# Order of the first loads, and one repeated weight load, in a two-problem attention kernel

## The chip, the cores and the metric

The kernel runs on one core of a Trainium2 chip. The metric is the device time of one execution in microseconds (us); lower is better. Times are medians over several runs unless a profiled execution is named, which is a single run.

## The reference

Two problems of the same shape, A and B, are computed one after the other and their outputs are joined along the last axis. All tensors are bf16. Each has tokens x (16 x 32 x 1024), a key and a value cache (16 x 4 x 512 x 128) and two weight matrices.

```python
q = (x @ wq).reshape(B, Sq, Hq, Dh).transpose(0, 2, 1, 3)   # 32 heads of 128
k = jnp.repeat(k_cache, rep, axis=1)                        # 4 kv heads, each for 8
v = jnp.repeat(v_cache, rep, axis=1)
scores = jnp.einsum("bhqd,bhkd->bhqk", q, k) * (Dh ** -0.5)
p = softmax(scores)
o = jnp.einsum("bhqk,bhkd->bhqd", p, v)
return o.transpose(0, 2, 1, 3).reshape(B, Sq, Hq * Dh) @ wo
```

## The kernel before

The 512 tokens of a problem (16 x 32) are four tiles of 128. The width of 1024 is eight chunks of 128 (`DC` = 8); `HC` is half of them, 4. There are 32 query heads in four groups of 8 (`REP`), one group for each key/value head.

**The head of the kernel** (L456 to L557) computes the queries of the first eight heads of problem A. It is the only stage in which the tensor engine has no other work. Six heads (`NF`) have their sums in PSUM first, the last two join later. The first four chunks of x are loaded as rows into `x_sb` and turned by tensor-engine transposes (`transpose_x`, L515, instructions at L519) with a copy out by VectorE for the one chunk and ScalarE for the other (L523); the last four chunks come through DMA transposes (`load_x_transposed`, L471). The weights of the eight heads come through `load_w0` (L477), piece by piece: first chunk 0 and chunk 1 of six heads, each 192 KB, from ScalarE's queue, then all others from SyncE's. The tokens are loaded by `load_x` (L465): two pieces of 128 KB (token tiles 0-1 and 2-3 of chunks 0 and 1), then one of 256 KB (chunks 2 and 3).

While these arrive, the tensor engine runs 23 matmuls on constants (`warm_up`, L509), whose result is not used. The written order after that is: transposes of the first half of the tokens, three more such matmuls, chunk 0 of three heads over the first half, transposes of the second half, chunk 0 of the other three heads, and so on (L537 to L557).

**What follows on SyncE's queue.** Behind the head's loads come block (0, 2) of the query weights, keys of group 0, block (0, 3), keys of group 1 and values of groups 0 and 1 (L496 to L501). A block `(pr, c4)` is 1 MB: all chunks of four heads, from head 4 x c4, of problem `pr`; `load_wq` (L242) allocates a new tile and enters it into `wq_tiles[pr, c4]`. The queue takes one DMA after another. Each DMA uses one of eight semaphores in turn, so that a DMA also waits for the one that used its semaphore last.

**The main loop** has 128 slots (i = 0 to 127), one for each pair of batch and key/value head of the two problems. A slot computes its scores (L358), the exponential on ScalarE (L366), sums on VectorE (L377) and, five slots later, the product with the values (L426). Between these the tensor engine takes about seven units of a stream of projection matmuls (`stream`, L559): eight units make a query head (L302), 32 make a tile of output (L321). Five units run before slot 0 (L576), and each slot runs 1, 5 and 1 of them, every fourth slot one less. Loads for later slots are entered in a plan and issued at the start of a slot (`at`, L581; `do_loads`):

```python
for c4 in range(3, 16):
    need = (c4 - 2) * 4 * DC / 7.0
    at(max(0, int(need) - 10), load_wq, c4 // 8, c4 % 8)
```

The order within each engine is written out by hand (`manual_schedule`); no scheduler moves instructions. Tiles of tag `blk` (20 buffers: weights, queries, transposed tokens, outputs of attention) are reused in turn.

Of the kernel before, what the change touches and what calls it, by code (L numbers as in the profile page):

```python
# [181 lines left out]
def kernel(  # L182
# [14 lines left out]
    nc = tc.nc  # L197
# [5 lines left out]
    TT = NTOK // P  # L203
# [14 lines left out]
    def fast_path(ok_i):  # L218
        with ExitStack() as fctx:
# [22 lines left out]
            def load_wq(pr, c4, eng=None, parts=((0, 4),)):  # L242
                t = blk_tile([P, DC, 4 * DH], "wq_sb")
                v = problems[pr][3].rearrange("(c p) n -> p c n", p=P)
                for a, b in parts:
                    (eng or nc.sync).dma_start(  # L246
                        out=t[:, :, a * DH:b * DH],
                        in_=v[:, :, (c4 * 4 + a) * DH:(c4 * 4 + b) * DH],
                    )
                wq_tiles[pr, c4] = t  # L250
# [205 lines left out]
            NF = REP - 2  # L456
# [8 lines left out]
            def load_x(d0, t0, t1):  # L465
                nc.sync.dma_start(
                    out=x_sb[:, t0:t1, d0 * P:(d0 + 2) * P],
                    in_=x_v[:, t0:t1, d0 * P:(d0 + 2) * P],
                )

            def load_x_transposed(d0):  # L471
                nc.sync.dma_start_transpose(  # L472
                    out=xT[0][:, d0:d0 + 2, :],
                    in_=A_x.flatten_outer_dims()[:, d0 * P:(d0 + 2) * P],
                )

            def load_w0(eng, d0, d1, h0, h1):  # L477
                eng.dma_start(  # L478
                    out=w0[d0 // HC][:, d0 % HC:(d1 - 1) % HC + 1, h0 * DH:h1 * DH],
                    in_=wq_v[:, d0:d1, h0 * DH:h1 * DH],  # L480
                )

            load_w0(nc.scalar, 0, 1, 0, NF)
            load_x(0, 0, TT // 2)
            load_w0(nc.scalar, 1, 2, 0, NF)
            load_x(0, TT // 2, TT)
            load_x(2, 0, TT)
            load_w0(nc.sync, 2, 3, 0, NF)
            load_w0(nc.sync, 3, 4, 0, NF)
# [2 lines left out]
            load_x_transposed(HC)  # L492
            load_w0(nc.sync, HC + 2, DC, 0, REP)
            load_x_transposed(HC + 2)
            nc.scalar.preload_act_table_set("natural_log_exp_and_others")
            load_wq(0, 2)  # L496
            load_k(0)
            load_wq(0, 3)
# [82 lines left out]
            def at(slot, fn, *args):  # L581
                plan.setdefault(slot, []).append((fn, args))

            for j in range(2, 2 * NG // GRP):
                at(GRP * (j - 1), load_k, j)
                at(GRP * (j - 1) + 2, load_v, j, 2 if j < 5 else 1)
            for c4 in range(3, 16):
                need = (c4 - 2) * 4 * DC / 7.0
                at(max(0, int(need) - 10), load_wq, c4 // 8, c4 % 8)

# [72 lines left out]
    ok_i = flag.tile([1, 1], I32, name="ok_i")  # L663
    total = 2 * 2 * NG * QW
    ok = fast_path(ok_i)
    with tc.If(ok < total, preferred_fallthrough_block=True, label="general"):
        general_path(tc, problems, out_flat)
# [30 lines left out]
```

## Time and profile before

| | us |
|---|---|
| median of 9 runs | 347.45 (347.17 to 349.38) |
| the profiled execution | 347.56 |
| its span, first to last instruction | 345.8 |
| tensor engine busy | 337.2 |
| vector engine busy | 266.4 |
| ScalarE busy | 186.1 |

In the profile PE is the tensor engine's matmuls, PEld its weight loads, DVE is VectorE, ACT is ScalarE, POOL is GpSimd and SP is SyncE; SPq and ACTq are the DMA issues of the last two. Times within the span count from its start. The row of slices divides the span into 40 parts of 8.6 us, each digit a share in tenths. A DMA's time to landing counts from the start of its issue to the arrival of its completion. SyncE's queue is shown by these lines of the timeline (start, duration of the issues, what, count):

```profile
0.86 1.48 SPq L466 DMA_DIRECT2D x_sb<-in_A_x_dram  x3
2.38 2.23 SPq L478 DMA_DIRECT2D w_sb<-in_A_wq_dram  x4
4.65 2.30 SPq L472 DMA_TRANSPOSE xT<-in_A_x_dram  x1
7.00 0.57 SPq L478 DMA_DIRECT2D w_sb<-in_A_wq_dram  x1
7.61 2.50 SPq L472 DMA_TRANSPOSE xT<-in_A_x_dram  x1
10.16 0.58 SPq L246 DMA_DIRECT2D wq_sb<-in_A_wq_dram  x1
```

ScalarE issues its two weight DMAs at 0.82 and 1.28 us, and its table load runs from 1.76 for 1.28 us.

### The profile page before, as it was taken

What the parts mean: (1) busy time and instruction counts of PE and PEld (TensorE: products, weight loads), DVE (VectorE), ACT (ScalarE), POOL (GpSimd) and SP (SyncE); (2) the same over time, 40 slices, a digit from 0 to 9 for tenths busy, and PEclk for the clock granted to TensorE, in tenths of its full rate; (3) what the DMA queues carried; (4) which work ended last, traced back from release to release, by engine and by line L of the source; (5) the groups of instructions that cost most, each with busy time, mean ns of one, the idle gap of its engine ahead of it and who ended that gap; (6) DMA issues with size and microseconds to landing.
All of it is one profiled execution on the core that took longest, in us unless ns stands there. A gap on an engine that the chain in (4) does not pass through costs nothing.

```text
span 345.8 us, 5471 instructions
## 1 busy us (share of the span) xinstructions
PE 337.2 (98%) x2089; PEld 214.9 (62%) x2128; DVE 266.4 (77%) x336; ACT 186.1 (54%) x209; POOL 46.7 (14%) x206
## 2 busy tenths in 40 slices
PE   7998999999999999999999999999999999999996
PEld 6454666666666666666666666666666666666555
DVE  0046788888888988888888888889888888889540
ACT  2046666676676666667655545554555555554110
POOL 0001001111111111110012112221222100111100
PEclk9999999999999999999999999999999999999999
DMA  7999979799999999999999955998449996440001
GB/s 237 281 224 353 259 216 269 171 258 261 307 258 228 239 223 220 216 238 306 265 273 258 242 138 139 351 275 218 118 108 300 335 204 146 91 124 0 17 17 33
DMA packets 127949, 72.75 MB, mean 210 GB/s; under 512 B 75824, under 2 KB 127152, under 8 KB 127920
## 3 DMA queue, kind: packets, MB, share of 16 engines
q1 hardware_dynamic: 127104, 70.86, 84.4%
q0 software_dynamic: 384, 1.05, 0.8%
q10 hardware_dynamic: 432, 0.46, 0.5%
q8 instruction: 17, 0.28, 0.3%
q14 instruction: 12, 0.10, 0.1%
HBM read 51.90 MB, written 2.10 MB: 156 GB/s over the span
## 4 chain that ended last, share of the span: by engine, by line
PE 89%; SPq 6%; DMA 3%; issue 1%; ACT 0%; ACTq 0%
PE f_ps L321 31%; PE q_ps L302 25%; PE ob L426 17%; PE s_ps L358 16%; SPq L276 3%; DMA wq_sb<-in_A_wq_dram 2%; SPq L472 1%; DMA x_sb<-in_A_x_dram 1%; SPq L246 0%; SPq L287 0%; SPq L478 0%; ACT o_sb L330 0%; SPq L693 0%; ACTq L330 0%
## 5 line engine op out<-in xcount | busy, mean ns | idle before, releaser
L366 ACT ACTIVATE p_sb<-s_ps,shift 128x1024 bf16<-128x1024 f32 x128 | 142.7, 1115 | 101.5 <-PE s_ps L358 85.0
L377 DVE TRANSPOSE_TENSOR_REDUCE parts<-p_sb 128x32 f32<-128x1024 bf16 x128 | 158.9, 1242 | 20.4 <-ACT p_sb L366 18.6
L321 PE MATMUL f_ps<-wo_sb,oT 128*128 128x512 bf16 (+1 forms) x525 | 127.5, 366 | 0.6
L302 PE MATMUL q_ps<-xT,wq_sb 128*128 128x512 bf16 x430 | 113.7, 379 | 2.0 <-DMA wq_sb<-in_A_wq_dram 1.4
L426 PE MATMUL ob<-p_sb,v_sb 128*128 128x256 bf16 x512 | 76.8, 273 | 0.8
L358 PE MATMUL s_ps<-qT,kT 128*128 128x256 bf16 x512 | 76.8, 273 | 0.0
L321 PEld LDWEIGHTS <-oT 128*128 128x128 bf16 x544 | 53.2, 98 | 36.0
L358 PEld LDWEIGHTS <-kT 128*128 128x128 bf16 x512 | 56.8, 113 | 28.4 <-issue 0.3
L302 PEld LDWEIGHTS <-wq_sb 128*128 128x128 bf16 x448 | 43.8, 98 | 33.2 <-DMA wq_sb<-in_A_wq_dram 1.7
L426 PEld LDWEIGHTS <-v_sb 128*128 128x128 bf16 x512 | 50.1, 98 | 20.0
L448 DVE TENSOR_TENSOR oT<-r,ob 128x512 bf16<-128x512 f32 x64 | 43.9, 687 | 23.2 <-PE ob L426 22.7
L412 DVE STREAM_TRANSPOSE r<-rall 128x512 f32<-128x512 f32 x64 | 44.2, 691 | 1.1
L310 ACT CAST qT<-q_ps 128x512 bf16<-128x512 f32 x56 | 32.7, 583 | 13.8 <-PE q_ps L302 13.8
L395 POOL COPY half<-cs 64x32 f32<-64x32 f32 x32 | 6.5, 204 | 231.9 <-DVE cs L385 231.8
L330 ACT CAST o_sb<-f_ps 128x512 bf16<-128x512 f32 (+1 forms) x17 | 9.5, 559 | 24.4 <-PE f_ps L321 16.7
L529 PE MATMUL q_ps<-xT,w_sb 128*128 128x512 bf16 (+1 forms) x68 | 15.9, 395 | 0.1
L385 DVE TENSOR_REDUCE cs<-parts 128x32 f32<-128x128 f32 x32 | 12.1, 377 | 1.1
L529 PEld LDWEIGHTS <-w_sb 128*128 128x128 bf16 x70 | 7.5, 109 | 7.2 <-issue 0.3
L407 DVE RECIPROCAL rall<-sums 128x32 f32<-128x32 f32 x32 | 10.2, 319 | 1.6 <-POOL sums L404 1.6
L554 DVE CAST qT<-q_ps 128x512 bf16<-128x512 f32 x4 | 2.8, 692 | 9.6 <-PE q_ps L529 9.5
L332 POOL DMA_DIRECT2D out_dram<-o_sb x8 | 4.6, 574 | 33.2 <-ACT o_sb L330 33.1
L396 POOL TENSOR_TENSOR half<-half,cs 64x32 f32<-64x32 f32 x32 | 7.8, 243 | 2.6
(25 smaller groups left out, 46.4 us busy)
## 6 DMA issues: line engine op xcount, KB each, us to landing
wq_sb<-in_B_wq_dram SPq DMA_DIRECT2D x8, 1024.0 KB, 6.2
wo_sb<-in_A_wo_dram SPq DMA_DIRECT2D x8, 1024.0 KB, 7.6
v_sb<-in_B_v_cache_dram SPq DMA_DIRECT2D x16, 512.0 KB, 4.6
wo_sb<-in_B_wo_dram SPq DMA_DIRECT2D x8, 1024.0 KB, 8.5
wq_sb<-in_A_wq_dram SPq DMA_DIRECT2D x7, 1024.0 KB, 6.2
v_sb<-in_A_v_cache_dram SPq DMA_DIRECT2D x13, 512.0 KB, 4.4
v_sb<-in_A_v_cache_dram SPq DMA_DIRECT2D x6, 256.0 KB, 4.5
w_sb<-in_A_wq_dram SPq DMA_DIRECT2D x2, 512.0 KB, 5.7
```

The lines of the kernel that those rows point to most:

```text
L276: nc.sync.dma_start_transpose(out=kT[:, q, :], in_=ks[q])
L302: nc.tensor.matmul(ps[:], lhsT=w[:, dc, (h % 4) * DH:(h % 4 + 1) * DH], rhs=xT[pr][:, dc, :], start=(dc == 0), stop=(dc == DC - 1),)
L310: nc.scalar.copy(out=qT[pr, g][:, :, hl, :], in_=ps[:].rearrange("p (b s) -> p b s", s=SQ),)
L321: nc.tensor.matmul(ps[:, 0:width], lhsT=oT[pr, tt][:, h, :], rhs=wo_tiles[pr, nh, h // REP][:, h % REP, off:off + width], start=(h == 0), ...
L358: nc.tensor.matmul(s_ps[:, c, :], lhsT=kT[:, i % GRP, c, :], rhs=qT[pr, g][:, b, :, :].rearrange("p h s -> p (h s)"), start=True, stop=True,)
L366: nc.scalar.activation(out=p_sb[:], in_=s_ps[:], func=ACTF.Exp, bias=shift[:], scale=SCALE)
L377: nc.vector.tensor_reduce(out=parts[k][:, q, :, :].rearrange("p c h -> p (c h)"), in_=st[i]["p"][:].rearrange("p c (h s) -> p (c h) s", s=SQ),
L385: nc.vector.tensor_reduce(out=cs[:], in_=parts.pop(k)[:].rearrange("p q c h -> p q h c"), axis=AX.X, op=ALU.add,)
L412: nc.vector.transpose(out=r[:].rearrange("p n s -> p (n s)"), in_=rall[:, k, o * 2 * REP:(o + 1) * 2 * REP] .unsqueeze(2).to_broadcast([P, ...
L426: nc.tensor.matmul(ob[j][:, q, :], lhsT=v_sb[:, i % GRP, c, :], rhs=st[i]["p"][:, c, :], start=(c == 0), stop=(c == KC - 1),)
L448: nc.vector.tensor_tensor(out=out, in0=rcp.pop(j)[:].rearrange("p (q h) s -> p q h s", h=REP), in1=ob.pop(j)[:].rearrange("p q (h s) -> p ...
L529: nc.tensor.matmul(first_q[h][:, ts], lhsT=w0[dc // HC][:, dc % HC, h * DH:(h + 1) * DH], rhs=xT[0][:, dc, ts], start=(dc == 0 and t0 == 0 ...
```

## The change

The order of the first loads changes, the table load of ScalarE moves ahead of its DMA, and the loop of planned weight loads starts at block 4 instead of block 3. Chunk 0's weights now come from SyncE in two pieces of three heads, 96 KB each, one behind each half of the tokens. Chunk 1's weights stay on ScalarE's queue, now behind the table load. Everything else on SyncE's queue keeps its order. The matmuls and their order are the same.

```diff
-            load_w0(nc.scalar, 0, 1, 0, NF)
+            nc.scalar.preload_act_table_set("natural_log_exp_and_others")
             load_x(0, 0, TT // 2)
+            load_w0(nc.sync, 0, 1, 0, NF // 2)
+            load_x(0, TT // 2, TT)
+            load_w0(nc.sync, 0, 1, NF // 2, NF)
             load_w0(nc.scalar, 1, 2, 0, NF)
-            load_x(0, TT // 2, TT)
             load_x(2, 0, TT)
             load_w0(nc.sync, 2, 3, 0, NF)
             load_w0(nc.sync, 3, 4, 0, NF)
...
             load_x_transposed(HC)
             load_w0(nc.sync, HC + 2, DC, 0, REP)
             load_x_transposed(HC + 2)
-            nc.scalar.preload_act_table_set("natural_log_exp_and_others")
             load_wq(0, 2)
...
-            for c4 in range(3, 16):
+            for c4 in range(4, 16):
                 need = (c4 - 2) * 4 * DC / 7.0
                 at(max(0, int(need) - 10), load_wq, c4 // 8, c4 % 8)
```

## The prediction, made before the changed kernel was run

> **What bounds the kernel now.** I read the page first, for the share of each engine and for the slices in which TensorE (PE) is not at 9 or 10 tenths.
>
> ```profile
> span 345.8 us, 5471 instructions
> PE 337.2 (98%) x2089; PEld 214.9 (62%) x2128; DVE 266.4 (77%) x336; ACT 186.1 (54%) x209; POOL 46.7 (14%) x206
> ...
> PE   7998999999999999999999999999999999999996
> ...
> PEclk9999999999999999999999999999999999999999
> ```
>
> PE is the bound: 98% of the span, and only the first slice, the fourth (26 to 35 us) and the tail are below 9. A change can pay only where PE stands still or runs slowly. The diff touches the first 25 us of loads and one later load, so I read next the waits of the first 40 us, then the chain that ended last in the same stretch.
>
> ```profile
> PEld L302 <- DMA wq_sb<-in_A_wq_dram: 1.7, 1, 1.7
> PE q_ps L302 <- DMA wq_sb<-in_A_wq_dram: 1.4, 1, 1.4
> PEld L519 <- DMA x_sb<-in_A_x_dram: 1.4, 1, 1.4
> PE xT_ps L519 <- DMA x_sb<-in_A_x_dram: 1.1, 1, 1.1
> ```
>
> ```profile
> 0.86 3.76 DMA x_sb<-in_A_x_dram
> ...
> 24.72 7.78 DMA wq_sb<-in_A_wq_dram
> 32.55 1.69 PE q_ps L302 x7
> ```
>
> (Start, duration, what.) PE waits for two transfers: at the start for the first tokens, issued at 0.86 and landed at 4.62; and at 31 us for query weights issued at 24.72 and landed at 32.50. Which weights? Five units run before slot 0 (L576) and 27 in slots 0 to 3, 32 in all, which are heads 8 to 11. Slot 4 opens head 12, block (0, 3). L498 has loaded that block already; the loop at L587 loads it again at slot 0 (need is 4.6, less 10 is below 0) into a new tile, and `wq_tiles[0, 3]` then names the second. The first copy, issued at 17.64, landed 5.7 us later, at 23.3, and is never read.
>
> The third thing stands in the timeline of the head, PE rows alone.
>
> ```profile
> 4.66 0.61 PE L519 MATMUL xT_ps<-ident,x_sb 128*128 128x128 bf16 x4 [1.10 <-DMA x_sb<-in_A_x_dram]
> ...
> 6.03 0.63 PE L519 MATMUL xT_ps<-ident,x_sb 128*128 128x128 bf16 x4
> ...
> 9.59 0.61 PE L519 MATMUL xT_ps<-ident,x_sb 128*128 128x128 bf16 x8
> ...
> 10.25 11.82 PE L529 MATMUL q_ps<-xT,w_sb 128*128 128x512 bf16 x53
> ```
>
> Four transposes take 0.6 us before 9.5 us, eight take the same after. Instruction starts read singly are 0.107 us apart for 128 columns, 0.213 for 256, 0.427 for 512 up to about 9.5 us, and 0.215 for 512 after it. So PE works at half speed until 9.5 us, which neither the idle columns nor PEclk (10 tenths throughout) tell.
>
> [...]between 2.4 and 2.8 us ScalarE's queue (q10) had the engines and SyncE's (q1), issued 0.04 us after it, almost nothing.
>
> ```profile
> q10 hardware_dynamic: 57, 0.09, 104.6%
> q1 hardware_dynamic: 6, 0.00, 2.5%
> ```
>
> **The change, part by part.**
>
> The second load of block (0, 3) goes: 1 MB and one SyncE issue. Head 12 then reads the first copy. The last s_ps matmul before the stall starts at 30.56 and four of 0.109 end at 31.0; the next matmul starts at 32.55. So 1.55 us goes. The first copy lands at 23.3 plus the shift below, about 24, and is needed at 28.8 at the earliest: it is no new wait.
>
> The tokens lead. The first half (256 packets of 512 B) landed at 4.62 behind and between ScalarE's 384 KB. ScalarE's first transfer, issued at 0.82, had bytes at 1.9. If SyncE's first one is alone, its bytes start at about 2.0; q1 alone moved 238 packets in the 0.4 us from 4.4, the ramp is slower (30 packets in 1.9 to 2.4), so 0.9 to 1.1 us and done by 3.0; from its last packets (about 4.0) to landing (4.62) it took 0.65. That gives 3.7, estimated; bounds 3.4 and 4.6 (no gain). The weights for three heads follow (128 packets): about 4.05, needed 0.78 us after the tokens (5.44 less 4.66), at 4.5. Second half of tokens: 4.5, needed at 5.1 (6.03 less 4.66 after the start). Other three heads: 4.9 to 5.4 with ScalarE's weights between, needed at 5.5. Second chunk from ScalarE: issued at 2.1 if behind the table load, landing 3.4 to 3.9 later as in before, at most 6.1; needed at 6.8. So nothing else is late there.
>
> What an earlier start is worth: at half speed, a start earlier by D is worth D/2 for an unchanged doubling, and a doubling earlier by D is worth D/2. The start goes from 4.66 to 3.7: 0.48 us. The warm-up's last matmul starts at 3.24 and streams until 3.35; the gap shrinks from 1.3 to 0.35 us.[...]
>
> The table load moves ahead of a DMA instead of behind two: it ends at about 2.1 instead of 3.04, and ScalarE's first copy is at 5.31. Cost nothing, also when that copy comes 1 us earlier.
>
> SyncE gets two more issues in front of everything. A step takes 0.45 plus 0.04 us (three in 1.48), nine of them before the first DMA transpose instead of seven: it starts at 0.86 + 9 x 0.48 = 5.2 instead of 4.65, where 0.4 us of waiting goes. All that follows on SyncE shifts by 0.55 us until the removed load. Against PE 2.2 us earlier in the head and 3.75 from slot 4 on:
> - transposed tokens, first pair: 4.65 + 6.3 becomes 11.5; first used after 23 matmuls of 0.215 from 10.0, at 14.9, now 12.7. Slack 1.2.
> - second pair: 7.61 + 5.7 becomes 13.9; used at 18.4, now 16.2.
> - block (0, 2): 10.16 + 6.2 becomes 16.9; used at 21.7, now 19.5.
> - first values: 23.55 + 5.3 becomes 29.4; used at 34.7, now 31.0. Slack 1.6.
> - third group of keys: 29.67 + 9.4 = 39.1; one MB less ahead at the 350 GB/s of this stretch is 3.0 us, plus 0.55: 36.6; used at 41.17 (slot 8), now 37.4. Slack 0.8, the smallest: this is what is late next, if anything.
> Later loads have more (slot 12's keys land at 44.1 for 50.5), and PE runs without gaps to the end, so what is won in front stays.
>
> Sum: 1.55 + 0.48 + 1.7 = 3.7 us. The profiled run took 347.56 (span 345.8 and 1.76 around it), 0.1 above the median 347.45. 347.5 less 3.7: 343.8.
>
> **The rivals.**
> - The speed does not double earlier. [...]ScalarE's DMA is issued beside the table load at 0.9, and its 192 KB take the engines first as before; the tokens then have q10's second transfer less against them and land at about 4.25. Gain 1.55 + 0.2 to 0.5: 345.5 to 345.8. For it: [...]q10's lead above.[...]
> - A new wait takes part of the gain: the keys of slot 8 land 1 us later than reckoned, or the first values do. It can take only what is over the slack, 0.5 to 1 us: 344.5.
> - Slower: the lead does not help and the split hurts. If SyncE's first bytes keep to 2.7 us and the tokens to 4.6, the three-head pieces and the second tokens line up behind one another on one queue with ScalarE's weights between, each some 0.5 us late for PE. [...]1.7 us lost, with 0.5 of waits: 2.2 against 1.55 gained, 348.2. It decides once the pieces land over 1 us after they are needed. Against it: the bytes before PE's first use are fewer than before.
> - That the change doesn't do what it says: only the delay behind the table load may fail, which is the first rival. The removed load is certain.
>
> **How the numbers follow.** Forecast (343.3 to 344.3) 0.43; speed not earlier (345.2 to 346.1) 0.40; new wait 0.08; slower 0.05; the rest, a gain below 0.7 us, 0.04. The range 343.2 to 346.1 leaves out about a tenth at each end. A change of 0.2% is 0.7 us, about what a measurement of this kernel can tell. Faster 0.91, same 0.05, slower 0.04.
>
> **What would show it.** In the changed profile: no wait of L302 on wq_sb near slot 4 (1.55 us); the first transpose at 3.7; ScalarE's one weight DMA at 2.1 (right) or 0.9 (first rival); transposes or 512-wide matmuls at the double rate from about 6 us (right) or 9.5; the first score matmul of slot 0 2.2 us before 22.98; slot 8 without a wait on kT. I am wrong if the first tokens still land after 4.2 us, or a wait on w_sb or x_sb appears before 10 us.

## The result, and the profile after

The changed kernel takes 345.90 us (median of 10 runs, 345.02 to 346.46) against 347.31 (30 runs): a ratio of 0.9952, 95% interval 0.9942 to 0.9963, or 1.4 us less. A second sample of six runs gave 345.75 and a ratio of 0.9946 (0.9926 to 0.9966). The forecast was 3.7 us less, so less than half of the gain came. The time lies where the first rival put it (345.5 to 345.8 as worked out, 345.2 to 346.1 as its range). The range on record, 343.2 to 346.1, holds the time only because it takes in that rival.

The page of the changed kernel, profiled at 346.26 us:

```profile
span 344.5 us, 5471 instructions
...
PE   7999999999999999999999999999999999999996
...
PE 97%; DMA 1%; issue 1%; ACT 0%; SPq 0%; ACTq 0%
```

The 8 in the fourth slice has become a 9, and the chain that ended last is now 97% tensor engine (89% before, where SyncE's queue had 6% and DMA 3% of it). The wait at 31 us is gone. Now the head, from the timeline (start, duration, engine, line, what, count, idle time before it):

```profile
0.82 1.28 ACT L483 ACT_TABLE_LOAD   x1 [0.82 <-PEq L683]
...
0.85 0.42 ACTq L478 DMA_DIRECT2D w_sb<-in_A_wq_dram  x1
0.86 0.45 SPq L466 DMA_DIRECT2D x_sb<-in_A_x_dram  x1
...
4.60 0.61 PE L520 MATMUL xT_ps<-ident,x_sb 128*128 128x128 bf16 x4 [1.05 <-DMA x_sb<-in_A_x_dram]
...
9.60 0.87 PE L520 MATMUL xT_ps<-ident,x_sb 128*128 128x128 bf16 x8
...
10.52 11.82 PE L530 MATMUL q_ps<-xT,w_sb 128*128 128x512 bf16 x53
```

(Behind the first loads, lines are one higher than before: L519 is now L520.) ScalarE's DMA, described ahead as standing behind the table load, starts 0.03 us after the table load, not 1.28 us later, and 0.01 us ahead of SyncE's first: it is not behind anything. The first transpose starts at 4.60 (4.66 before), with 1.05 us of idling ahead of it. Eight transposes take 0.87 us: half speed until about 10.1 us, even later than in the run before (9.5). The queues from 2.4 to 2.8 us (packets, MB, share of the engines) tell why the tokens are late:

```profile
q10 hardware_dynamic: 57, 0.09, 97.6%
q1 hardware_dynamic: 19, 0.01, 8.0%
```

This is the picture of before: ScalarE's 192 KB run first, and the tokens on SyncE's queue follow.

Where the 1.30 us between the two profiled runs are is read at one place: the first projection matmul of slot 4 (head 12) starts at 31.27 instead of 32.55, 1.28 us earlier, and PE is dense from there on in both. That start is the measure for everything below.

### The profile page after: what moved, and what is told of

It is laid out like the page before. It is cut to its first block, busy times and chain, and to the rows that moved or that the text cites. A ratio compares the mean times of both kernels' runs of the same rounds, so it can differ in the third digit from the quotient of the medians.

```text
span 344.5 us, 5471 instructions
## 1 busy us (share of the span) xinstructions
PE 337.4 (98%) x2089; PEld 215.2 (62%) x2128; DVE 266.2 (77%) x336; ACT 186.1 (54%) x209; POOL 46.7 (14%) x206
## 3 DMA queue, kind: packets, MB, share of 16 engines
q0 software_dynamic: 384, 1.05, 0.8%
## 4 chain that ended last, share of the span: by engine, by line
PE 97%; DMA 1%; issue 1%; ACT 0%; SPq 0%; ACTq 0%
PE f_ps L321 31%; PE q_ps L302 27%; PE ob L426 17%; PE s_ps L358 16%; PE q_ps L530 5%; DMA x_sb<-in_A_x_dram 1%; PE xT_ps L520 0%; ACT o_sb L330 0%; PE q_ps L512 0%; SPq L694 0%; ACTq L330 0%
## 5 line engine op out<-in xcount | busy, mean ns | idle before, releaser
L358 PE MATMUL s_ps<-qT,kT 128*128 128x256 bf16 x512 | 76.8, 273 | 0.0
L358 PEld LDWEIGHTS <-kT 128*128 128x128 bf16 x512 | 56.8, 113 | 28.4 <-issue 0.3
L407 DVE RECIPROCAL rall<-sums 128x32 f32<-128x32 f32 x32 | 10.2, 318 | 1.6 <-POOL sums L404 1.6
```

Of the source, the lines that this page charges most:

```text
L358: nc.tensor.matmul(s_ps[:, c, :], lhsT=kT[:, i % GRP, c, :], rhs=qT[pr, g][:, b, :, :].rearrange("p h s -> p (h s)"), start=True, stop=True,)
L407: nc.vector.reciprocal(out=rall[:, k, :], in_=quad.pop(k)[:])
```

## The experiments

All are variants of the two kernels. Ratios are to the kernel before on the same chip. "Tokens" is the start of the first transpose, "doubling" the time from which matmuls start at double the rate (worked out from the starts around it), "slot 4" the start of its first projection matmul, all from each kernel's one profiled run.

| kernel | median us | ratio (95%) | tokens | doubling | slot 4 | profiled run us |
|---|---|---|---|---|---|---|
| before | 347.3 | 1 | 4.66 | 9.5 | 32.55 | 347.56 |
| changed | 345.90 | 0.9952 (0.9942 to 0.9963) | 4.60 | 10.1 | 31.27 | 346.26 |
| changed, again | 345.75 | 0.9946 (0.9926 to 0.9966) | 4.43 | 9.9 | 31.07 | 346.19 |
| removal alone | 346.44 | 0.9973 (0.9962 to 0.9984) | 4.76 | 10.2 | 31.37 | 346.44 |
| removal alone, again | 346.12 | 0.9970 (0.9959 to 0.9980) | 4.78 | 7.8 | 30.23 | 345.30 |
| order alone | 351.74 | 1.0144 (1.0126 to 1.0161) | 4.54 | 7.6 | 33.36 | 348.80 |
| before, 34 warm-up matmuls | 349.32 | 1.0040 (1.0018 to 1.0061) | 4.93 | 3.6 | 32.60 | 347.61 |
| changed, 34 warm-up matmuls | 345.56 | 0.9959 (0.9942 to 0.9976) | 4.54 | 5.8 | 29.32 | 344.87 |
| held behind the table load | 344.74 | 0.9934 (0.9918 to 0.9951) | 3.35 | 5.2 to 6.2 | 29.22 | 344.54 |
| held for GpSimd | 344.80 | 0.9925 (0.9906 to 0.9944) | 3.35 | 6.0 | 29.38 | 344.39 |
| all on SyncE | 344.71 | 0.9919 (0.9898 to 0.9939) | 3.35 | 3.6 | 28.79 | 343.94 |
| all on SyncE, block loaded twice | 351.81 | 1.0127 (1.0107 to 1.0147) | 3.35 | 5.5 | 33.93 | 352.17 |

Except in the last row, where the clock falls back later, the profiled time less the start of slot 4 is the same within about 0.6 us, over starts from 28.79 to 33.36: 347.56 less 32.55 is 315.0, 343.94 less 28.79 is 315.2, 345.30 less 30.23 is 315.1. The largest remainder, 315.6 with 34 warm-up matmuls in the changed kernel, goes with two new waits for keys, which hold up the weight loads of the scores (L358) for 0.5 us at slot 8 (the smallest slack of the prediction) and for 0.6 us at 66.25 us. A still faster head has its next limit there.

**The removal alone.** The kernel before, with

```diff
-            for c4 in range(3, 16):
+            for c4 in range(4, 16):
```

> The kernel before, with only the repeated load of block (0, 3) taken out. Theory A: the whole gain of the change (1.4 us) is this removal, so about 345.8 us, within 0.3 of the changed kernel, and no wait of L302 on wq_sb at 31 us. Rival B: the new order of the first loads carries a part of 0.5 us or more; then this kernel stays at 346.3 or above.

It took 346.44 us, 0.9 less than before (0.27%, 0.16 to 0.38). The wait is gone; in the timeline:

```profile
9.76 0.82 PE L519 MATMUL xT_ps<-ident,x_sb 128*128 128x128 bf16 x8
...
31.37 1.67 PE L302 MATMUL q_ps<-xT,wq_sb 128*128 128x512 bf16 x7
```

Theory A, that it carries all of the gain, doesn't hold by its number: 346.44 is above the 346.3 named for rival B. Once more, since the difference is small:

> The removal alone once more, to size it: 346.4 (0.9 us under the kernel before) within 0.3 if the first sample of seven runs was typical; 345.8 if it was the draw, and the order of the first loads is then worth nothing. In the profile: no wait at 31 us, tokens at 4.6 to 4.8 us, the speed doubling at 9.5 to 10.2 us.

346.12 us, 0.30% less than before (0.20 to 0.41). The two samples agree: the removal alone is worth about 1.0 us, not 1.4 and not the 1.55 of my sum. The kernel before has a reason to hide the difference: it restarts when the second load lands, at 32.5 us, whenever PE gets there. What the removal gives is that time less PE's arrival, and the arrival moves with the doubling. The run profiled before had one at 9.5 us and was ready at 31.0; the two of the removal had 10.2 and 7.8 us and reached slot 4 at 31.37 and 30.23.

**The order alone.** The changed kernel, with the loop from block 3 again.

> The changed order of the first loads, with block (0, 3) still loaded twice. Theory A: no gain from the order, 347.3 us within 0.4, tokens landing at about 4.6 us as before, and the wait at 31 us back with 1 to 2 us (the queue is 0.6 us later). Rival B: 346.8 or below. Third: the queue shift makes the wait longer than the tokens gain, 347.8 or above.

351.74 us (four runs, 348.80 to 353.26). That is on the side of the third theory (347.8 or above), but far more than a later queue explains. In the waits of the first 60 us:

```profile
PE q_ps L302 <- DMA wq_sb<-in_A_wq_dram: 3.2, 1, 3.2
```

SyncE's two more issues move the second load of block (0, 3) from 24.72 to 25.64 and its landing from 32.50 to 33.3, and with it the whole rest: 0.8 us. That explains about 348.1, not 351.7. The three runs above 351 have a mean granted clock of 0.990 to 0.995, the profiled one 0.998, and its clock is full at slot 4. No trace of the three was kept; the last experiment shows, in a kernel with a longer wait, what probably happened there.

**The DMA really held behind the table load.** One line in the changed kernel:

```diff
             load_w0(nc.sync, 0, 1, NF // 2, NF)
+            nc.scalar.copy(out=w0[0][:, 1, 0:1], in_=shift[:])
             load_w0(nc.scalar, 1, 2, 0, NF)
```

> The changed kernel, with one tiny ScalarE copy (one column of the weight tile, overwritten by the load) between the table load and ScalarE's weight DMA, so that this DMA cannot be issued before the table load is over (about 2.3 us instead of 0.85). Theory A: the tokens were late because ScalarE's 192 KB ran ahead of them; now they land at 3.4 to 3.9 us instead of 4.56. [...]the speed doubles at about 6 us and the time is 344.0; if it does not, the earlier start alone gives 345.2 to 345.6. Rival C: the tokens land at 4.5 us even alone, since the first bytes of SyncE's queue are slow, and the time stays at 345.9.

344.74 us. The tokens landed at 3.15 us (2.3 us after their issue, 3.7 in the changed kernel), earlier than I had reckoned for a lone transfer. The timeline, and below it one line of the chain that ended last (start, duration):

```profile
2.33 0.38 ACTq L478 DMA_DIRECT2D w_sb<-in_A_wq_dram  x1
...
3.35 0.63 PE L521 MATMUL xT_ps<-ident,x_sb 128*128 128x128 bf16 x4
...
6.18 1.80 PE L531 MATMUL q_ps<-xT,w_sb 128*128 128x256 bf16 x12 [0.81 <-DMA w_sb<-in_A_wq_dram]
...
2.33 3.80 DMA w_sb<-in_A_wq_dram
```

From 2.4 to 2.8 us SyncE's queue now has the engines to itself:

```profile
q1 hardware_dynamic: 163, 0.09, 78.2%
```

Rival C is out; theory A holds for the tokens. The time lies between its two cases (344.0 and 345.2). There is no gap after the warm-up, and PE then waits 0.8 us, until 6.18. The twelve matmuls behind that wait (nine of 256 columns, three of 512) start in 1.64 us, where half speed needs 3.2, so the speed doubled during the wait, between 5.2 and 6.2 us. I took the wait for one on chunk 1's weights, held too long. It is not: the nine matmuls are chunk 0's, and what landed at 6.13 is chunk 0's second piece, which SyncE issued at 2.33, the moment at which ScalarE issued chunk 1's. It took 3.8 us; with no DMA from ScalarE (two kernels below) it takes 2.6. So the held transfer again made SyncE's transfer beside it late. On the mistaken reading I held chunk 1's weights less, by a GpSimd memset (issue at 1.47 us):

```diff
+            nc.gpsimd.memset(w0[0][:, 1, 0:1], 0.0)
+            load_w0(nc.scalar, 1, 2, 0, NF)
             load_x(0, 0, TT // 2)
...
-            load_w0(nc.scalar, 1, 2, 0, NF)
```

> The changed kernel, with a GpSimd memset of one column of the weight tile, which ScalarE's weight DMA waits for (it overwrites that column): the DMA is issued at about 1.6 us, between 0.85 (changed kernel) and 2.33 (held behind the table load). Theory A: SyncE's first tokens are still ahead and land at 3.2 to 3.6 us, and the chunk-1 weights land about 0.7 us earlier than in the run held behind the table load, so its wait of 0.8 us on w_sb goes: 343.9 to 344.4. Rival H: the tokens are late again (4.4 us), 345.6 to 346.

344.80 us, short of what theory A had: the tokens are first again and the wait of 0.8 us is gone, but another has come.

```profile
4.86 0.82 PE L531 MATMUL q_ps<-xT,w_sb 128*128 128x256 bf16 x3 [0.56 <-DMA w_sb<-in_A_wq_dram]
```

Now it is the first piece of chunk 0 that is late. SyncE issued it at 1.36, 0.11 us ahead of ScalarE's transfer, and it took 3.5 us to land, against 2.2 in the run before. So it is not the earlier issue that puts ScalarE's transfer ahead. And the same without any DMA from ScalarE:

```diff
-            load_w0(nc.scalar, 1, 2, 0, NF)
+            load_w0(nc.sync, 1, 2, 0, NF)
```

> The changed kernel with chunk 1's weights on SyncE's queue too, behind the second piece of chunk 0, and none from ScalarE. Theory A: tokens alone at the front, landing at 3.2 us; chunk 1's weights land at 5.5 to 6 us, so PE waits about 0.5 us for them; all later loads are 0.5 us later: 344.3 to 345. Rival: SyncE's extra issue makes the last loads of the head late (a wait of PE on w_sb or xT between 10 and 16 us), 345.5 or above.

344.71 us. The three do not differ by more than their intervals; all are 0.6 to 1.2 us under the changed kernel. The last one's profile is what the forecast meant: slot 4 starts at 28.79, where the forecast had 28.8, though PE waits 0.4 us for chunk 1's weights at 6.55, as expected. The median of its six runs is still 0.9 us above the 343.8 forecast. Its timeline:

```profile
3.35 0.50 PE L520 MATMUL xT_ps<-ident,x_sb 128*128 128x128 bf16 x4
...
3.69 0.34 PE L512 MATMUL q_ps<-const-bfloat16-1.0 128*128 128x128 bf16 x3
...
7.83 12.03 PE L530 MATMUL q_ps<-xT,w_sb 128*128 128x512 bf16 x55
```

Three constant matmuls in 0.34 us, 0.53 in the kernel before: the speed doubled at 3.6 us. The 512-wide matmuls start at 7.83 instead of 10.25.

**Is it the gap that delays the doubling?** The changed kernel with more warm-up, tokens left late:

```diff
-            warm_up(23)
+            warm_up(34)
```

> The changed kernel with 34 instead of 23 matmuls on constants before the first transpose: 11 more of 0.107 us fill the gap until the tokens land at 4.56. Theory D: the idle gap is what keeps the speed from doubling[...], 344.2 to 345.0 us. Rival E: the doubling does not depend on the gap, or it needs real work: 345.9 to 346.1 us, half speed until about 10 us.

Two rows of its timeline:

```profile
5.88 0.39 PE L520 MATMUL xT_ps<-ident,x_sb 128*128 128x128 bf16 x4
...
8.36 12.03 PE L530 MATMUL q_ps<-xT,w_sb 128*128 128x512 bf16 x54
```

With the gap filled the doubling comes at 5.8 us, with tokens at 4.54. Theory D holds for the profile (344.87). The median of 345.56 lies between the two theories and is hardly below the changed kernel's (345.90 and 345.75): the 22 runs reach from 343.91 to 348.75, seven of them are at 346.06 to 346.80, no faster than with the gap, and three, all above 348, have a granted clock of 0.995. No trace of those ten was taken, and where they lost it stays open. Over the profiled runs: with a gap of about 1 us before the tokens the speed doubled at 9.5, 10.1, 9.9, 10.2, 7.8 and 7.6 us; with no gap before them at 5.8, between 5.2 and 6.2, at 6.0, 3.6 and 5.5; and at 3.6 in the kernel of the next experiment, before its gap. It is not at a fixed time in either group, but the two don't overlap. In four of the five without a gap the tokens came earlier too; only the changed kernel with 34 warm-up matmuls changes the gap alone. So the gap is the likely cause for the profiled runs, and not shown as the cause of the times of the others. How much idling it takes was not measured finely: a wait of 0.56 us at 4.3 to 4.9 us did not keep the speed from doubling at 6.0.

**What a faster head is worth before the removal.** The kernel before, with the same 34 warm-up matmuls.

> The kernel before, with 34 instead of 23 matmuls on constants, so that the tensor engine has no gap before the tokens and its speed doubles earlier in most runs. Theory F: before, the time is pinned by the second load of block (0, 3), which lands at 32.5 us whatever the head does; a faster head only makes the wait at slot 4 longer, 3 to 4 us instead of 1.4, so 347.3 us within 0.3 at best.[...] Rival G: a faster head is worth what it saves, 345.5 to 346.5.

```profile
4.93 0.40 PE L519 MATMUL xT_ps<-ident,x_sb 128*128 128x128 bf16 x4 [0.64 <-DMA x_sb<-in_A_x_dram]
...
32.60 1.69 PE L302 MATMUL q_ps<-xT,wq_sb 128*128 128x512 bf16 x7 [3.12 <-DMA wq_sb<-in_A_wq_dram]
```

PE is 1.7 us earlier at slot 4 and waits that much longer: 32.60 as before, 347.61 us. Theory F holds. The median of 20 runs is 349.32, slower than before; 12 of them, at 348.86 to 350.93, have a granted clock of 0.990 to 0.995. None of these has a trace. The last experiment makes the wait longer than any, the fastest head with block (0, 3) loaded twice:

> The kernel with all first weights on SyncE's queue, which was the fastest (344.7), with block (0, 3) loaded twice again. Theory F: the second load lands about 1 us later than before (33.5 us) and the tensor engine is there 3 us earlier, so it stands for about 5 us at slot 4, and the records show it at half speed[...]: 350 to 353 us. Rival: the clock is not touched, and the time is that of the landing alone, 348.2 to 348.6.

351.81 us. Busy time in stretches of 1 us (PE, PEld, DVE, ACT, POOL with counts; then the granted clock, the DMA share and GB/s):

```profile
28.00:29.00 1.00, 0.99 (x7) 0.50 (x5) 0.56 (x1) 0.82 (x2) 0.00 (x0) 1.00 1.09 381
29.00:30.00 1.00, 0.00 (x0) 0.00 (x0) 0.97 (x2) 1.00 (x2) 0.00 (x0) 1.00 1.09 381
...
32.00:33.00 1.00, 0.00 (x0) 0.00 (x0) 0.97 (x2) 0.00 (x0) 0.00 (x0) 0.89 1.10 351
33.00:34.00 1.00, 0.07 (x1) 0.07 (x2) 0.04 (x1) 0.00 (x0) 0.00 (x0) 0.50 1.09 348
34.00:35.00 1.00, 1.00 (x3) 0.36 (x4) 0.00 (x0) 0.00 (x0) 0.00 (x0) 0.50 1.08 347
...
39.00:40.00 1.00, 1.00 (x6) 0.44 (x4) 0.86 (x1) 0.58 (x2) 0.00 (x0) 0.70 1.28 270
40.00:41.00 1.00, 1.00 (x8) 0.66 (x7) 0.38 (x1) 0.00 (x0) 0.00 (x0) 1.00 1.33 261
```

PE stands from 29.0 to 33.93. At about 32.8 (0.89 is 0.22 us at 0.50) the clock drops to half, and comes back at about 39.6 (0.70 is 0.6 us at 0.50). From 33.93 to 39.6 PE works at half speed: 2.8 us lost. With the landing 1.4 us later than before, that makes 4.2 of the 4.6 us by which this profiled run is over the one before. This is what the removal protects: with the block loaded twice, the kernels with a new order of loads (order alone and this one) are slower than the kernel before, and without the second load they are faster.

## Why the prediction was wrong

- **"The tokens lead ... If SyncE's first one is alone": failed.** It was not alone. The forecast's term of 0.48 us rested on ScalarE's DMA issued "at 2.1 if behind the table load"; it was issued at 0.85, with the table load running from 0.82 to 2.10. In the profile before no DMA stood behind a table load, so the delay was an estimate from the words of the change alone, and I gave them a little more weight (0.43) than the first rival's issue at 0.9 (0.40). The tokens came 0.06 us earlier instead of 0.96. The run with the DMA held confirms that a lone first transfer is early: then they come at 3.35. It also shows that the forecast was too good had the delay worked: its time is 344.74, not 343.8. The term "Other three heads: 4.9 to 5.4 with ScalarE's weights between" was wrong: they landed at 6.13, and PE waited 0.8 us. The prediction's two queue lines show one queue with nearly all of the engines (104.6% against 2.5%), and a ScalarE transfer held until 2.33 us still delayed the one beside it (3.8 us to landing instead of 2.6).
- **"1.7" in the sum, for a speed that doubles earlier: failed with it.** The 1.7 us was my estimate, as was the slower rival's "1.7 us lost"; no trace showed either. The profile before has one doubling, at 9.5 us. In the changed kernel the gap stayed at 1.05 us, and the doubling came at 10.1. The gap as the cause fits the two groups of profiles above, and in them it is the larger part of what the order could give; a gap of 0.35 us, on which the forecast rested, never occurred. And one profile gives no schedule: the doubling lies anywhere between 7.6 and 10.2 with a gap and between 3.6 and 6.2 without, and one kernel, the removal alone, doubled at 10.2 in one profile and at 7.8 in the other.
- **"So 1.55 us goes": the wait went, the size was that of one run.** Measured with the removal alone, 0.9 and 1.2 us by the medians. The term is the restart at 32.55 less PE's arrival (31.0 in the run profiled before), and so it isn't independent of the other two: the sum is right only as one difference at slot 4, 32.55 to 31.27. In the changed kernel's profile PE is at slot 4 only at 31.27: its doubling is 0.6 us later than in that run, which at half speed costs 0.3.
- SyncE's queue: shift of all that follows reckoned at 0.55, found between 0.65 (block (0, 2) issued at 10.81 instead of 10.16) and 1.4 (first values, 24.98 instead of 23.55). SyncE's wait in the head for the semaphore of the DMA eight before is 0.3 us (0.4 in the kernel before). No new wait came of it in the changed kernel, neither on the keys of slot 8 nor on the first values, but PE also came later than forecast. The table load cost nothing, as forecast: it ends at 2.10, and ScalarE then has nothing to do for 3.15 us.
- The first rival had the right step (issue at 0.9, measured 0.85), but its tokens were to land at 4.25 and landed at 4.56, and its gain of 1.75 to 2.05 us was 1.28 in the profiles. That the median comes within 0.1 us of that rival's estimate is in part luck.
- The slower rival (pieces late, 348.2) didn't occur in the changed kernel. Late pieces did cost 0.6 and 0.8 us in the two kernels with ScalarE's DMA held. A stall that costs the clock is seen at slot 4 with the block loaded twice and all on SyncE.

The changed kernel is 0.2% below the removal alone (0.9952 and 0.9946 against 0.9973 and 0.9970), about 0.7 us with an uncertainty of half of that. Its tokens come 0.2 to 0.3 us earlier than there, which at half speed is worth 0.1 to 0.2; whether the rest is the draw of the doubling was not settled.

## What to carry to other kernels

A wait that is removed is worth its end less the arrival of the work, and a gain ahead of such a wait was worth nothing here until it went (32.60 against 32.55 with a faster head): read both from one place, the first instruction after it. The order in the source was not the order on the chip here: the DMA written behind the table load on the same engine started 0.03 us after it, and waited only when it depended on a result (issued at 2.33 us behind a one-column copy, at 1.47 behind a memset). In the first microseconds of a kernel, ask which other transfers are issued beside the one that is needed first: the tokens took 3.7 us to land beside ScalarE's transfer and 2.3 without it. An idle gap of the tensor engine can go with a loss of more than its length: in the profiles here the speed doubled at 7.6 to 10.2 us with a gap of about 1 us and at 3.6 to 6.2 without, and after a wait of 4.9 us PE worked at half speed from 33.93 to 39.6 us.

## What was not expected of the hardware

- Of two transfers issued within 0.01 us on two queues, one took 98% of the engines from 2.4 to 2.8 us: ScalarE's 192 KB made SyncE's 128 KB land 3.7 us after issue instead of 2.3. Being issued first is not the reason, as a piece of SyncE's issued 0.11 us ahead was late too (3.5 instead of 2.2). Whether the queue, the size or the larger packets (1536 B against 512 B for the tokens) decide was not tested.
- A wait of 4.9 us put the tensor engine at half speed for 6.8 us, from 3.8 us after its last matmul; the kernels with waits of 3.1 and 3.2 us in the profile had a clock of 0.990 to 0.995 and times of 348.86 to 353.26 in other executions, but no fall at that wait in the profiled one.
- The granted clock of the profile shows that fall, but reads 1.00 throughout the half speed of the first microseconds; only the starts of the matmuls show it.
